# A retention kernel with two MLPs behind it: query multiplications and decay tables issued a block ahead, a converted piece's parts a block behind

## The chip, the cores and the metric

The kernel runs on one core of a Trainium2 chip. The metric is the device time of one execution in microseconds (us), the median of several. PE is the matrix engine, DVE the vector engine, ACT the scalar engine, POOL the GpSimd engine; SP only issues transfers.

## What is computed

The reference, cut to its core:

```
def _attn_ref(q, k, v):                      # 2 x 8 heads x 768 x 64, fp32
    gamma = 1.0 - 2.0 ** (-5.0 - np.arange(H))
    for t in range(S):
        state = gamma * state + einsum('bhd,bhe->bhde', k[:, :, t], v[:, :, t])
        y[:, :, t] = scale * einsum('bhd,bhde->bhe', q[:, :, t], state)

x = y.transpose(0, 2, 1, 3).reshape(1536, 512)
x = ((x @ w_a) * (x @ w_b)) @ w_out          # d_ff 1536
h = x @ w_in                                 # d_ff 2048
out = (h * sigmoid(1.702 * h)) @ w_out2
```

The weights come as float64 and the kernel converts them to two float32 parts (hi and lo); activations are split in two parts as well, and each product is the sum of three.

## The kernel before

**Retention.** The two sequences of 768 rows are cut into 12 blocks of 128 rows, `SEQ` = 6 to a sequence. For block n the kernel does this:

- `att_load(n)`: two transfers of 512 KB on SP's queue, `qv` (queries, values) and `kk` (keys in two layouts). Four buffers (`RAWBUFS`) each; iteration n issues the load of block n+4, and in some iterations also a 512 KB weight piece (`w_dma`).
- `att_q(n)`: POOL multiplies the queries with a decay table `qdec[c]`, c = n % 6. Table 1 is loaded; the others are made from it by `att_qdec(c)`, four ACT instructions with the factors `gdec[c]`, which POOL writes at the start with 64x1 memsets.
- `att_v(n)`: POOL multiplies the values with `vdec[c]`.
- `att_scores(n)`: PE, `ps_sc` from `kk` and q; then DVE masks them into `a`.
- `att_kv(n)`: PE adds block n's keys times values to `ps_kv`; then ACT copies that to `state`. The last block of a sequence has none.
- `att_av(n)`: PE, `a` times v (L204) and, except in a sequence's first block, `state` times q (L216); then ACT rounds the result to `xh`, and DVE takes the rest to `xl`.

Each engine runs its instructions in the order in which the program issues them (the schedule is manual). In iteration n that order is: scores(n+1), v(n+1), kv(n), the decay table of block n+2, one conversion step, av(n), q(n+2), the load of block n+4.

**Conversion during the retention.** Three weight pieces (`EARLY`) are converted in blocks 2 to 10, one step to a block: `w_bits`, `w_sign`, `w_add` on DVE, and with the third step `w_parts`: ACT rounds `wt` to `wh`, POOL takes the rest to `wl`.

**Start.** 11 small products on zeros (`warm`) keep PE occupied until the first data, then scores(0), then 8 more. Block 0's load is cut into four transfers of 256 KB, which go, with the decay tables and the mask, to SP's and ACT's queues.

**MLPs.** `layer(1)` and `layer(2)` follow; their first product (L342) is issued right behind the last av. Nothing in them is touched.

The buffers' waits come from the framework. Transfers take turns on eight completion semaphores, so that one is issued only when the eighth before it has landed.

Of the kernel before, what the change touches and what calls it, by code (L numbers as in the profile page):

```python
# [7 lines left out]
F32 = mybir.dt.float32  # L8
# [5 lines left out]
ALU = mybir.AluOpType  # L14

P = 128
B, H, S, D = 2, 8, 768, 64
NP = H // 2
# [6 lines left out]
SEQ = S // P  # L25
# [15 lines left out]
def retention_moe_kernel(  # L41
# [9 lines left out]
    nc = tc.nc  # L51
# [9 lines left out]
    attp = retention.enter_context(tc.tile_pool(name="attp", bufs=2))  # L61
    ps_att = retention.enter_context(tc.tile_pool(name="ps_att", bufs=1, space=PSUM))

    def lo_part(engine, lo, src, hi):
        engine.tensor_tensor(out=lo, in0=src, in1=hi.bitcast(F32), op=ALU.subtract)  # L65
# [5 lines left out]
    causal = attp.tile([P, 1, P], F32, tag="causal", name="causal", bufs=1)  # L71
# [9 lines left out]
    def att_load(n):  # L81
        if n >= NBLK:
            return
        qv, kk = (attp.tile([P, 2, DM], F32, tag=t, name=t, bufs=RAWBUFS) for t in ("qv", "kk"))
        if n == 0:
            nc.sync.dma_start(out=qv[:, 0, :], in_=att[n][:, 0, :])
            nc.scalar.dma_start(out=kk[:, 0, :], in_=att[n][:, 1, :])
            nc.scalar.dma_start(out=causal[:, 0, :], in_=cmask[:, 0:P])
            nc.scalar.dma_start(
                out=vdec[:, 0].rearrange("p h o -> p (h o)"), in_=cdec[:, NP * P:NP * P + H]  # L90
            )
            nc.sync.dma_start(out=qv[:, 1, :], in_=att[n][:, 3, :])
            nc.scalar.dma_start(out=kk[:, 1, :], in_=att[n][:, 2, :])
            nc.scalar.dma_start(out=qdec[:, 1].rearrange("p a t -> p (a t)"), in_=cdec[:, 0:NP * P])
        else:
            nc.sync.dma_start(out=qv, in_=att[n][:, 0:4:3, :])
            nc.sync.dma_start(out=kk, in_=att[n][:, 1:3, :])
        qv_t[n], kk_t[n] = qv, kk

    def att_constants():  # L100

        gamma = [1.0 - 2.0 ** (-5.0 - h) for h in range(H)]
        for c in range(1, SEQ):
            for h in range(H):
                nc.gpsimd.memset(vinv[:, c, h, :], gamma[h] ** (-float(P) * c))  # L105
        for c in range(SEQ):
            for h in range(H):
                rows = slice(64 * (h % 2), 64 * (h % 2) + 64)
                nc.gpsimd.memset(gdec[rows, c, h // 2:h // 2 + 1], gamma[h] ** (float(P) * (c - 1)))  # L109

    def att_vdec():

        nc.vector.tensor_scalar(
            out=causal, in0=causal, scalar1=0.0, scalar2=1.0, op0=ALU.is_gt, op1=ALU.mult
        )
        for c in range(1, SEQ):
            nc.gpsimd.tensor_tensor(out=vdec[:, c], in0=vdec[:, 0], in1=vinv[:, c], op=ALU.mult)  # L117

    def att_qdec(c):

        if c < SEQ and c != 1:
            for p in range(NP):
                nc.scalar.activation(
                    out=qdec[:, c, p], in_=qdec[:, 1, p], func=ACTF.Copy, scale=gdec[:, c, p:p + 1]
                )

    def att_q(n):
        if n < NBLK:
            t = attp.tile([P, NP, P], F32, tag="q", name="q", bufs=3)
            (nc.vector if n == 1 else nc.gpsimd).tensor_tensor(  # L130
                out=t, in0=qv_t[n][:, 0, :].rearrange("p (a t) -> p a t", t=P), in1=qdec[:, n % SEQ], op=ALU.mult
            )
            q_t[n] = t

    def att_v(n):
        if n < NBLK:
            t = attp.tile([P, H, D], F32, tag="v", name="v")
            nc.gpsimd.tensor_tensor(  # L138
                out=t,
                in0=qv_t[n][:, 1, :].rearrange("p (h d) -> p h d", d=D),  # L140
                in1=vdec[:, n % SEQ].to_broadcast([P, H, D]),
                op=ALU.mult,
            )
            v_t[n] = t
# [53 lines left out]
    def att_av(n):  # L198
        c = n % SEQ
        ps = ps_att.tile([P, NP, P], F32, tag="av", name="ps_av", bufs=2)  # L200
        for p in range(NP):
            for h2 in range(2):
                h = 2 * p + h2
                nc.tensor.matmul(  # L204
                    ps[64 * h2:64 * h2 + 64, p, :],
                    v_t[n][:, h, :],
                    a_t[n][:, NP * h2 + p, :],
                    start=(p == 0),
                    stop=(c == 0),
                    skip_group_check=True,  # L210
                )
        if c > 0:
            for p in range(NP):
                for h2 in range(2):
                    rows = slice(64 * h2, 64 * h2 + 64)
                    nc.tensor.matmul(  # L216
                        ps[rows, p, :],
                        state_t[n][rows, p, :],
                        q_t[n][rows, p, :],
                        start=False,  # L220
                        stop=True,
                        skip_group_check=True,
                    )
        hi, lo = (t[:, :, n * P:(n + 1) * P] for t in x)
        if n == 0:
            t = attp.tile([P, NP, P], F32, tag="q", name="x0", bufs=3)
            nc.vector.tensor_tensor(out=t, in0=ps, in1=qdec[:, 0], op=ALU.mult)
            ps = t
        nc.scalar.copy(hi, ps)
        lo_part(nc.vector, lo, ps, hi)  # L230
# [10 lines left out]
    is_down = [j == 3 - ph for ph, f, j in pieces]  # L241
    wraw, wt, whl = {}, {}, {}
    nxt = {"dma": 0, "split": 0}
    room = {False: WUP, True: WDOWN}
    stage = [None, None, None]

    def w_dma():
        i = nxt["dma"]
        if i >= len(pieces):
            return  # L250
        nxt["dma"] += 1
        ph, f, j = pieces[i]
        t = rawp.tile([P, DM, 2], I32, tag="wraw", name="wraw", bufs=4)
        src = (w1 if ph == 1 else w2)[f][:, j, :]
        nc.sync.dma_start(out=t.rearrange("p a b -> p (a b)"), in_=src.bitcast(I32))
        wraw[i] = t
# [3 lines left out]
    def w_carry(i):  # L260
        low, high = wraw[i][:, :, 0], wraw[i][:, :, 1]
        wt[i] = rawp.tile([P, DM], F32, tag="wt", name="wt", bufs=3)
        nc.scalar.activation(out=wt[i], in_=high.bitcast(F32), func=ACTF.Abs)  # L263
        nc.scalar.activation(out=low, in_=low.bitcast(U32), func=ACTF.Copy, scale=2.0 ** -29)  # L264
# [19 lines left out]
    def w_parts(i):  # L284
        t = wt.pop(i)
        pool = wdown if is_down[i] else wup
        whl[pieces[i]] = hi, lo = [pool.tile([P, DM], F32R, tag=x, name=x) for x in ("wh", "wl")]
        nc.scalar.copy(hi, t)  # L288
        lo_part(nc.gpsimd, lo, t, hi)
# [18 lines left out]
    def w_early(n):  # L308

        i, k = divmod(n - 2, 3)  # L310
        if i < 0 or i >= EARLY:
            return
        (w_bits, w_sign, w_add)[k](i)
        if k == 2:
            w_dma()
            w_parts(i)
            room[is_down[i]] -= 1
            nxt["split"] += 1

    def w_points(n):  # L320
        for _ in range(n):
# [137 lines left out]
    def warm(ps, n):  # L459

        for _ in range(n):
            nc.tensor.matmul(ps[:, 0, :], zero, zero, start=True, stop=True)

    with tc.manual_schedule():
        nc.vector.memset(zero, 0.0)
        att_constants()
        for n in range(RAWBUFS):
            att_load(n)
        ps = ps_att.tile([P, NP, P], F32, tag="av", name="ps_warm", bufs=2)
        warm(ps, WARM)  # L470
        att_v(0)
        att_vdec()
        att_scores(0)
        att_q(1)
        warm(ps, 8)
        for n in range(NBLK):
            if n > 0:
                att_scores(n + 1)
            att_v(n + 1)
            att_kv(n)  # L480
            if n < SEQ:
                att_qdec(n + 2 if n else 0)
                if n == 0:
                    att_qdec(2)
            w_early(n)
            att_av(n)
            if n == 0:
                att_scores(1)
            att_q(n + 2)
            if n + RAWBUFS < NBLK:  # L490
                att_load(n + RAWBUFS)
            if n in (0, 1, 2, 9):
                w_dma()
            if n % 3 == 1 and n // 3 < EARLY:
                w_carry(n // 3)
        layer(1)
        layer(2)
# [66 lines left out]
```

## Time and profile before

| | us |
|---|---|
| Median of 3 runs | 626.16 (625.23 to 626.41) |
| The profiled execution's own time | 626.12 |
| Its span | 624.3 |
| PE busy in the span | 607.0 (97%) |
| DVE, ACT, POOL busy | 371.7, 237.1, 150.0 |
| First product of the MLPs starts at | 64.09 |

The span is what the profiler saw between the first and the last instruction; 1.8 us of the execution's own time lie around it. In the chain of work that ended last, PE has 93% and POOL 3%. The busy share is a mean over stages: the stage that the change touches is the retention, the first 64 us.

### The profile page before, as it was taken

The numbers are of one execution on the slowest core, as the hardware profiler recorded it, in microseconds if no ns is written. First come the engines' busy times: TensorE is split into PE (matmuls) and PEld (weight loads), VectorE is DVE, ScalarE is ACT, GpSimd is POOL, SyncE is SP. The second block draws the span as 40 slices with busy tenths as digits, with TensorE's granted clock in tenths as the row PEclk, the third lists the DMA queues.
The fourth block names the chain that finished last, engine by engine and source line by source line (L and its number), as shares of the span: only waits on it lengthen the run. The fifth ranks groups of instructions, "written<-read, shape, count | busy, mean of one in ns | idle before, by whom it ended". The sixth has DMA issues, their size and how long they took to land.

```text
span 624.3 us, 7868 instructions
## 1 busy us (share of the span) xinstructions
PE 607.0 (97%) x3190; PEld 504.9 (81%) x3190; DVE 371.7 (60%) x414; ACT 237.1 (38%) x340; POOL 150.0 (24%) x187
## 2 busy tenths in 40 slices
PE   7888999999999999999999999999999999999996
PEld 6777888888888888888888888888888888888885
DVE  3554268776056777235887667842888377836422
ACT  2433244444134552034444265534554055314300
POOL 7455033323012323002332212220223022202000
PEclk9888999999999999999999999999999999999999
DMA  8973123225012333012331212131114102200022
GB/s 311 369 244 111 35 77 97 97 71 166 0 35 68 101 102 101 1 34 68 101 102 34 69 34 68 62 107 35 63 39 135 35 34 68 67 1 1 0 101 102
DMA packets 17043, 52.21 MB, mean 84 GB/s; under 512 B 1776, under 2 KB 1904, under 8 KB 17008
## 3 DMA queue, kind: packets, MB, share of 16 engines
q1 hardware_dynamic: 16288, 50.86, 24.9%
q10 hardware_dynamic: 720, 0.86, 0.4%
q8 instruction: 25, 0.41, 0.3%
q14 instruction: 10, 0.08, 0.0%
HBM read 48.57 MB, written 3.15 MB: 83 GB/s over the span
## 4 chain that ended last, share of the span: by engine, by line
PE 93%; POOL 3%; issue 3%; DVE 0%; DVEq 0%; POOLq 0%
PE ps L342 52%; PE ps L379 37%; PE ps_sc L159 1%; PE ps_av L204 1%; PE ps_av L216 1%; POOL v L138 1%; POOL q L130 1%; POOL gdec L109 1%; PE ps_kv L186 1%; POOL vinv L105 0%; DVE part L396 0%; POOL vdec L117 0%; DVEq L560 0%; POOL wl L65 0%; POOLq L138 0%
## 5 line engine op out<-in xcount | busy, mean ns | idle before, releaser
L65 POOL TENSOR_TENSOR wl<-wt,wh 128x512 fp32r<-128x512 f32 x68 | 117.0, 1725 | 410.1 <-ACT wh L288 385.1
L342 PE MATMUL ps<-xh,wh 128*128 128x512 f32 x480 | 128.9, 389 | 0.0
L342 PE MATMUL ps<-xl,wh 128*128 128x512 f32 x480 | 128.8, 389 | 0.0
L342 PE MATMUL ps<-xh,wl 128*128 128x512 f32 x480 | 128.8, 389 | 0.0
L342 PEld LDWEIGHTS ps<-xl,wh 128*128 128x128 f32 x480 | 90.1, 188 | 18.7
L342 PEld LDWEIGHTS ps<-xh,wh 128*128 128x128 f32 x480 | 90.0, 188 | 18.8 <-issue 0.2
L342 PEld LDWEIGHTS ps<-xh,wl 128*128 128x128 f32 x480 | 90.1, 188 | 18.7
L269 DVE TENSOR_SCALAR wt<-wt 128x512 f32<-128x512 f32 x68 | 63.8, 938 | 53.5 <-ACT wt L263 53.5
L359 ACT CAST gh<-sb 128x1536 fp32r<-128x1536 f32 (+1 forms) x42 | 44.1, 1051 | 112.6 <-DVE sb L358 106.2
L358 DVE TENSOR_TENSOR sb<-ps,sb 128x1536 f32<-128x1536 f32 (+1 forms) x42 | 51.3, 1220 | 48.8 <-ACT sb L442 24.4
L65 DVE TENSOR_TENSOR gl<-sb,gh 128x1536 fp32r<-128x1536 f32 (+1 forms) x42 | 51.5, 1226 | 47.1 <-ACT gh L359 47.1
L396 DVE TENSOR_TENSOR part<-ps,part 128x1536 f32<-128x1536 f32 (+1 forms) x24 | 35.5, 1487 | 48.4 <-PE ps L379 48.4
L288 ACT CAST wh<-wt 128x512 fp32r<-128x512 f32 x68 | 42.0, 617 | 42.1 <-DVE wt L282 42.1
L276 DVE SCALAR_TENSOR_TENSOR wt<-wraw,wt 128x512 int32<-128x512 int32 x68 | 55.7, 819 | 2.2
L379 PE MATMUL ps<-wl,gh 128*128 128x512 f32 x192 | 55.2, 389 | 0.0
L379 PE MATMUL ps<-wh,gh 128*128 128x512 f32 x192 | 55.2, 389 | 0.0
L379 PE MATMUL ps<-wh,gl 128*128 128x512 f32 x192 | 55.2, 389 | 0.0
L282 DVE CUSTOM_DVE_ANT_0 wt<-wraw,wt 128x1024 uint16<-128x1024 uint16 x68 | 50.6, 744 | 6.4
L263 ACT ACTIVATE wt<-wraw 128x512 f32<-128x512 f32 x68 | 45.7, 672 | 1.5 <-POOL wl L65 1.5
L264 ACT ACTIVATE wraw<-wraw 128x512 int32<-128x512 uint32 x68 | 45.2, 664 | 0.0
L442 ACT ACTIVATE sb<-ps 128x1536 f32<-128x1536 f32 (+1 forms) x24 | 23.8, 1029 | 54.1 <-PE ps L342 54.1
L436 ACT COPY sb<-ps 128x1536 f32<-128x1536 f32 x12 | 17.4, 1446 | 66.6 <-PE ps L342 66.6
(47 smaller groups left out, 559.9 us busy)
## 6 DMA issues: line engine op xcount, KB each, us to landing
wraw<-in_w_dram SPq DMA_DIRECT2D x68, 512.0 KB, 3.7
qv<-in_att_dram SPq DMA_DIRECT2D x11, 512.0 KB, 7.1
kk<-in_att_dram SPq DMA_DIRECT2D x11, 512.0 KB, 6.0
out_dram<-part SPq DMA_DIRECT2D x3, 768.0 KB, 3.6
out_dram<-part SPq DMA_DIRECT2D x3, 256.0 KB, 2.1
kk<-in_att_dram ACTq DMA_DIRECT2D x2, 256.0 KB, 5.2
qv<-in_att_dram SPq DMA_DIRECT2D x2, 256.0 KB, 4.4
qdec<-in_cdec_dram ACTq DMA_DIRECT2D x1, 256.0 KB, 6.3
```

The lines of the kernel that those rows point to most:

```text
L65: engine.tensor_tensor(out=lo, in0=src, in1=hi.bitcast(F32), op=ALU.subtract)
L263: nc.scalar.activation(out=wt[i], in_=high.bitcast(F32), func=ACTF.Abs)
L264: nc.scalar.activation(out=low, in_=low.bitcast(U32), func=ACTF.Copy, scale=2.0 ** -29)
L269: nc.vector.tensor_scalar(out=t, in0=t, scalar1=F64_LOW, scalar2=F64_HIGH, op0=ALU.max, op1=ALU.min)
L276: nc.vector.scalar_tensor_tensor(out=ti, in0=wraw[i][:, :, 1], scalar=-0x40000000, in1=ti, op0=ALU.bitwise_and, op1=ALU.bitwise_or)
L282: nc.vector.tensor_tensor(out=ti, in0=ti, in1=wraw.pop(i)[:, :, 0], op=ALU.add)
L288: nc.scalar.copy(hi, t)
L342: nc.tensor.matmul(ps[:, g, :], l, r, start=(i == 0 and k == 0), stop=(i == 2 and k == max(late or now)), skip_group_check=True,)
L358: nc.vector.tensor_tensor(out=sb[:, c], in0=ps[:, c], in1=sb[:, c], op=ALU.mult)
L359: nc.scalar.copy(gh[:, c], sb[:, c])
L379: nc.tensor.matmul(ps[:, n, :], l, r, start=(f == min(g_t) and i == 0), stop=(f == max(g_t) and i == 2), skip_group_check=True,)
L396: nc.vector.tensor_tensor(out=t[:, c], in0=ps[:, c], in1=t[:, c], op=ALU.add)
```

## The change

Nearly the same instructions are issued in another order.

- q(n+2) is issued ahead of v(n+1) and kv(n), not behind av(n), and the decay table of block n+3, not n+2, is made in iteration n. Table 2 is made before the loop, ahead of the first `state` copy on ACT.
- The tag `q` gets 4 buffers for 3, `v` 3 for 2.
- `gdec` is written in the order 2, 0, 3, 4, 5; table 1's 8 memsets are left out, since it is loaded. Only vdec 1 is made ahead of v(1), the other four behind q(2).
- `w_parts(i)` is issued one block behind `w_add(i)`, ahead of that block's av.
- The second half of block 0's `kk` goes to SP's queue, not ACT's.
- The second warm-up has 12 products, not 8.

```
             nc.sync.dma_start(out=qv[:, 1, :], in_=att[n][:, 3, :])
-            nc.scalar.dma_start(out=kk[:, 1, :], in_=att[n][:, 2, :])
+            nc.sync.dma_start(out=kk[:, 1, :], in_=att[n][:, 2, :])
...
-        for c in range(SEQ):
+        for c in (2, 0, 3, 4, 5):
...
-            t = attp.tile([P, NP, P], F32, tag="q", name="q", bufs=3)
+            t = attp.tile([P, NP, P], F32, tag="q", name="q", bufs=4)
...
-            t = attp.tile([P, H, D], F32, tag="v", name="v")
+            t = attp.tile([P, H, D], F32, tag="v", name="v", bufs=3)
...
         i, k = divmod(n - 2, 3)
+        if i > 0 and k == 0:
+            w_parts(i - 1)
+            room[is_down[i - 1]] -= 1
+            nxt["split"] += 1
         if i < 0 or i >= EARLY:
             return
         (w_bits, w_sign, w_add)[k](i)
         if k == 2:
             w_dma()
-            w_parts(i)
-            room[is_down[i]] -= 1
-            nxt["split"] += 1
...
-        att_vdec()
+        att_vdec([1])
...
         att_q(1)
-        warm(ps, 8)
+        att_qdec(2)
+        warm(ps, 12)
         for n in range(NBLK):
             if n > 0:
                 att_scores(n + 1)
-            att_v(n + 1)
+            if n == 0:
+                att_v(1)
+                att_q(2)
+                att_vdec(range(2, SEQ))
+            else:
+                att_q(n + 2)
+                att_v(n + 1)
             att_kv(n)
-            if n < SEQ:
-                att_qdec(n + 2 if n else 0)
-                if n == 0:
-                    att_qdec(2)
+            if n == 0:
+                att_qdec(0)
+            if n + 3 < SEQ:
+                att_qdec(n + 3)
             w_early(n)
             att_av(n)
             if n == 0:
                 att_scores(1)
-            att_q(n + 2)
```

ACT from its first computing instruction to block 1, before (`state` is the copy behind kv, L123 the decay tables, four instructions to a table, `xh` the rounding behind av):

```order
L195 ACT_TABLE_LOAD
L195 COPY state_251<-ps_kv_242 128x256
L123 ACTIVATE qdec_83<-qdec_83,gdec_82 128x128 x8
L229 CAST xh_85<-x0_270 128x4x128
L195 COPY state_314<-ps_kv_242 128x256
L123 ACTIVATE qdec_83<-qdec_83,gdec_82 128x128 x4
L229 CAST xh_85<-ps_av_320 128x4x128
```

The same place after the change (L120 are the decay tables, L192 the copy, L226 the rounding):

```order
L120 ACT_TABLE_LOAD
L120 ACTIVATE qdec_83<-qdec_83,gdec_82 128x128 x4
L192 COPY state_253<-ps_kv_244 128x256
L120 ACTIVATE qdec_83<-qdec_83,gdec_82 128x128 x8
L226 CAST xh_85<-x0_272 128x4x128
L192 COPY state_316<-ps_kv_244 128x256
L120 ACTIVATE qdec_83<-qdec_83,gdec_82 128x128 x4
L226 CAST xh_85<-ps_av_322 128x4x128
```

Four instructions (table 2) and the table load now stand ahead of the first copy of the state; the eight behind it are tables 0 and 3, where they were 0 and 2.

POOL from block 4 to the first converted piece, before (`qv_287`, `qv_341`, `qv_400` and `qv_455` are blocks 4, 5, 6 and 7; `wl_486` is the first piece's second part):

```order
L130 TENSOR_TENSOR q_398<-qv_287,qdec_83 128x512
L138 TENSOR_TENSOR v_417<-qv_287,vdec_80 128x512
L130 TENSOR_TENSOR q_453<-qv_341,qdec_83 128x512
L138 TENSOR_TENSOR v_470<-qv_341,vdec_80 128x512
L65 TENSOR_TENSOR wl_486<-wt_347,wh_485 128x512
L130 TENSOR_TENSOR q_508<-qv_400,qdec_83 128x512
L138 TENSOR_TENSOR v_528<-qv_400,vdec_80 128x512
L130 TENSOR_TENSOR q_551<-qv_455,qdec_83 128x512
```

After (`qv_287`, `qv_341`, `qv_400`, `qv_451` and `qv_502` are blocks 4 to 8):

```order
L127 TENSOR_TENSOR q_417<-qv_341,qdec_83 128x512
L135 TENSOR_TENSOR v_419<-qv_287,vdec_80 128x512
L127 TENSOR_TENSOR q_466<-qv_400,qdec_83 128x512
L135 TENSOR_TENSOR v_468<-qv_341,vdec_80 128x512
L127 TENSOR_TENSOR q_520<-qv_451,qdec_83 128x512
L135 TENSOR_TENSOR v_522<-qv_400,vdec_80 128x512
L65 TENSOR_TENSOR wl_525<-wt_347,wh_524 128x512
L127 TENSOR_TENSOR q_564<-qv_502,qdec_83 128x512
```

Each q stands one block further ahead of the v beside it, and the piece's part stands behind the q of block 7, where it stood ahead of the q of block 6.

## Rows read from the trace of the kernel before

**Rows 1.** Waits in 0 to 66 us: us in total, times, longest.

```profile
PE ps_sc L159 <- POOL q L130: 10.2, 6, 2.8
```

**Rows 2.** Timeline, late retention: start us, us, engine, line, operation [idle before <-releaser].

```profile
40.76 1.16 PE L159 MATMUL ps_sc<-q,kk 64*128 64x128 f32 x16
43.34 1.16 PE L159 MATMUL ps_sc<-q,kk 64*128 64x128 f32 x16
...
54.84 1.16 PE L159 MATMUL ps_sc<-q,kk 64*128 64x128 f32 x16
...
56.45 1.05 PE L204 MATMUL ps_av<-a,v 128*64 128x128 f32 x16
...
58.44 1.16 PE L159 MATMUL ps_sc<-q,kk 64*128 64x128 f32 x16
...
64.09 1.20 PE L342 MATMUL ps<-xh,wh 128*128 128x512 f32 x4
```

**Rows 3.** Timeline, block 2 of the retention.

```profile
20.19 1.16 PE L159 MATMUL ps_sc<-q,kk 64*128 64x128 f32 x16 [0.26 <-POOL q L130]
...
22.34 1.28 ACT L123 ACTIVATE qdec<-qdec,gdec 128x128 f32<-128x128 f32 x4
...
23.70 1.27 POOL L130 TENSOR_TENSOR q<-qv,qdec 128x512 f32<-128x512 f32 x1 [2.55 <-ACT qdec L123]
...
24.53 0.69 DVE L65 TENSOR_TENSOR xl<-ps_av,xh 128x512 fp32r<-128x512 f32 x1 [1.11 <-ACT xh L229]
...
25.02 1.16 PE L159 MATMUL ps_sc<-q,kk 64*128 64x128 f32 x16 [1.15 <-POOL q L130]
```

**Rows 4.** Timeline, POOL at the first converted piece.

```profile
33.60 1.27 POOL L65 TENSOR_TENSOR wl<-wt,wh 128x512 fp32r<-128x512 f32 x1 [2.81 <-ACT wh L288]
```

**Rows 5.** Windows: busy us by engine (instructions), granted clock, DMA share, GB/s.

```profile
16.00:17.00 1.00, 1.00 (x20) 0.92 (x19) 1.00 (x2) 0.00 (x0) 0.11 (x1) 0.50 1.03 414
20.00:30.00 10.00, 7.51 (x130) 6.44 (x132) 5.84 (x8) 6.05 (x15) 4.89 (x6) 1.00 1.00 357
```

**Rows 6.** Timeline, the first two blocks.

```profile
3.29 1.28 ACT L195 ACT_TABLE_LOAD   x1 [3.29 <-issue]
...
6.77 2.05 PE L462 MATMUL ps_warm<-zero 128*128 128x128 f32 x16
...
9.07 1.29 DVE L130 TENSOR_TENSOR q<-qv,qdec 128x512 f32<-128x512 f32 x1 [0.96 <-DMA qdec<-in_cdec_dram]
...
9.87 0.69 PE L186 MATMUL ps_kv<-v,kk 128*64 128x64 f32 x16 [1.05 <-POOL v L138]
...
13.86 1.35 DVE L65 TENSOR_TENSOR xl<-x,xh 128x512 fp32r<-128x512 f32 x1 [0.98 <-ACT xh L229]
...
14.71 1.44 PE L159 MATMUL ps_sc<-q,kk 64*128 64x128 f32 x16 [2.19 <-POOL q L130]
15.13 2.34 DVE L167 TENSOR_TENSOR a<-ps_sc,causal 128x1024 f32<-128x1024 f32 x2
...
16.99 1.92 PE L204 MATMUL ps_av<-a,v 128*64 128x128 f32 x16
```

**Rows 7.** Timeline of SP's queue: three loads.

```profile
5.39 0.43 SPq L96 DMA_DIRECT2D qv<-in_att_dram  x1
...
7.18 0.53 SPq L97 DMA_DIRECT2D kk<-in_att_dram  x1
...
22.39 0.42 SPq L255 DMA_DIRECT2D wraw<-in_w_dram  x1
```

**Rows 8.** The same three in DMA views of their own: KB, us to landing.

```profile
qv<-in_att_dram SPq DMA_DIRECT2D x1, 512.0 KB, 6.2
...
kk<-in_att_dram SPq DMA_DIRECT2D x1, 512.0 KB, 9.4
...
wraw<-in_w_dram SPq DMA_DIRECT2D x1, 512.0 KB, 6.4
```

**Rows 9.** The page: a conversion step on DVE (busy, mean ns).

```profile
L276 DVE SCALAR_TENSOR_TENSOR wt<-wraw,wt 128x512 int32<-128x512 int32 x68 | 55.7, 819 | 2.2
```

More of the change, by code (lines that the diff above doesn't have):

```diff
@@ L109, in att_constants, with att_vdec @@
                 nc.gpsimd.memset(gdec[rows, c, h // 2:h // 2 + 1], gamma[h] ** (float(P) * (c - 1)))
[L111 to L116, printed above, removed]
+    def att_vdec(cs):
+        for c in cs:
             nc.gpsimd.tensor_tensor(out=vdec[:, c], in0=vdec[:, 0], in1=vinv[:, c], op=ALU.mult)
@@ L225, in att_av @@
         if n == 0:
-            t = attp.tile([P, NP, P], F32, tag="q", name="x0", bufs=3)
+            t = attp.tile([P, NP, P], F32, tag="q", name="x0", bufs=4)
             nc.vector.tensor_tensor(out=t, in0=ps, in1=qdec[:, 0], op=ALU.mult)
@@ L471, in retention_moe_kernel @@
         att_v(0)
-        att_vdec()
+        att_vdec([1])
+        nc.vector.tensor_scalar(
+            out=causal, in0=causal, scalar1=0.0, scalar2=1.0, op0=ALU.is_gt, op1=ALU.mult
+        )
         att_scores(0)
         att_q(1)
-        warm(ps, 8)
+        att_qdec(2)
+        warm(ps, 12)
         for n in range(NBLK):
```

## The prediction

> **What bounds the kernel now.** I read the chain of work that ended last first: nearly all of it is PE (the table above). So time can only come from stretches in which PE waits, or runs at the lower level of its clock. The waits of the first 66 us come next: six times PE waits for POOL's q ahead of the scores, 10.2 us in total [rows 1]. The timeline of the retention then shows three kinds of blocks; q(n), sc(n), kv(n), av(n) and so on are block n's.
>
> Late blocks run at PE's own pace: from sc(10) at 54.84 to sc(11) at 58.44 is 3.60 us; a block without the product with the state takes 43.34 - 40.76 = 2.58; from sc(11) to the first MLP product at 64.09 it is 5.65 [rows 2]. A block without kv I put at 3.0: 3.60 less 0.6, the kv row of 0.69 without its drain [rows 6].
>
> Blocks 3 to 5 are slower: from 20.19 to 25.02 is 4.83 us [rows 3]. The reader is to see a closed loop there: sc starts, kv follows, ACT copies the state and only then makes the next table (22.34, 1.28 us), POOL's q starts when that is done after idling 2.55, and PE's next sc starts when q is done after idling 1.15. PE's 3.6 us of work are part of a loop of 4.8.
>
> The third kind follows a converted piece: POOL idles 2.81 us for `wh`, with the next q queued behind that wait [rows 4]; PE's longest wait for a q is 2.8 [rows 1].
>
> The clock comes on top. Between 16 and 17 us the granted clock is 0.50, the 1.2 GHz level, after PE idled 2.19 us ahead of sc(2) [rows 5, 6]; from 20 to 30 us, with idle times of 1.15, it is 1.00, the 2.4 GHz level. The part L204 of av takes 1.92 us at the lower level [rows 6] and 1.05 at the upper [rows 2].
>
> The transfers are the next thing in line: from 20 to 30 us the DMA engines' share is 1.00 [rows 5]. kk(3) is issued at 7.18 and lands 9.4 later, at 16.58; the third weight piece is issued at 22.39 and lands 6.4 later, at 28.79 [rows 7, 8]. In SP's order that is the ninth transfer of 512 KB behind kk(3), so one takes (28.79 - 16.58) / 9 = 1.36 us.
>
> **The start.** ACT now loads its function table and makes decay table 2 ahead of the first state copy, and this waits for the loaded table 1. Before, DVE waited for that table until 9.07 [rows 6]. Were it still so, the copy could start at 9.07 + 1.28 (function table) + 1.28 (four activations) = 11.63; before, it started when kv(0), which started at 9.87, was through, about 10.6. That would be 1.0 us late. But `kk`'s half, 256 KB, no longer stands ahead of table 1 in ACT's queue, which at the rate above is worth 0.68 us: I take 11.63 - 0.68 = 10.95, 0.3 late, with bounds of 0 and 1.0. The Trainium skill has a rule against this (DMA: Bandwidth & Descriptors, section "Issuing engines are not separate DMA queues"): all issuers' transfers interleave on the same 16 engines, and another issuer saves only the issuing time. By that rule the gain here is one issue, some 0.4 us, and the copy 0.6 late; no run yet tells which. The final sum by it would be at most 0.3 us longer.
>
> SP's queue gets the half: qv(1) comes one issue and 0.68 us of transfer later. q(1), on DVE, waited for table 1 anyway, and sc(1) stands behind av(0), which ends near 9.87 + 0.5 + 1.05 = 11.4; q(1) would be ready near 10.4, a cover of 1 us. The four added warm-up products cost 4 x 2.05 / 8 = 1.0 us, which fits PE's wait ahead of kv(0), 1.05 us [rows 6]; the omitted memsets let POOL's v(0) come earlier, so the cover holds and kv(0) stays at 9.87.
>
> q(2) now stands ahead of the remaining vdec work and waits for qv(2), which lands at 5.39 + 6.2 = 11.59 [rows 7, 8] and for table 2 at 10.95: it ends at 11.65 + 1.27 = 12.92. kk(2), one transfer behind qv(2), lands at 12.95, and sc(2) starts then instead of at 14.71. PE does kv(1) and is through at 12.95 + 1.16 + 0.6 = 14.7. Next it needs a(1). Before, DVE started a(1) at 15.13 (two of them in 2.34 us) [rows 6], at the end of the sequence state copy, table 0, x0, xh(0), xl(0), which is not shortened: a(1) is ready at 15.13 + 1.17 + 0.3 = 16.6. That is the stall that takes over: PE idles 1.9 us and av(1) starts at 16.65, not 16.99.
>
> Does the clock fall here? 1.15 us of idling left it up, 2.19 let it fall; 1.9 is nearer to the second. I take the lower level for av(1): before, it took from 16.99 until PE went idle at 20.19 - 0.26, 2.94 [rows 3, 6]. So sc(3) is at 19.6, against 20.19 before; with the clock up av takes 3.60 - 1.16 - 0.6, some 1.9, and sc(3) is at 18.6.
>
> **Blocks 3 to 11.** Table c is made two iterations ahead of its sc and q one, so the loop of 4.8 is open; POOL's own work per block is 1.27 for q and, with v taken at the same, 2.5 in all, under 3.6. PE's pace then gives: sc(4) 23.2, sc(5) 26.8, sc(6) 30.4; block 5 has no kv, sc(7) 33.4; block 6 has no product with the state, sc(8) 36.0.
>
> The floor under it is the landing of kk. kk(4) to kk(8) are the 2nd, 5th, 8th, 11th and 14th transfer behind kk(3) (two weight pieces and more lie between): 19.3, 23.4, 27.5, 31.5, 35.6. Each is just ahead of PE. With the clock up from sc(3) PE would be at sc(8) at 35.0 and wait for 35.7. So both branches meet: sc(8) near 36.0. From there 3 x 3.60 + 5.65 = 16.45 to the first MLP product: 52.4, against 64.09.
>
> **The converted pieces.** `wh` is issued when its `wt` has been ready for a block, so POOL's wait of 2.81 is gone; `wl`'s own 1.27 us stay, hidden in POOL's slack of 3.6 - 2.5 and the block that q now lies ahead. Without that cover a block with a piece would cost 1.3 more. The third piece's rounding now precedes xh(11) on ACT, some 0.6 us later; the last columns of x are read last by the first MLP product, which hides it. The extra buffers cost nothing.
>
> **The sum.** The MLPs do what they did, shifted by 64.09 - 52.4 = 11.7 us. The profiled execution's 626.12 less 11.7 is 614.4 (its span 624.3 becomes 612.6); it lies at the median of the runs, so that stands for the median too.
>
> **Rivals.**
> Transfers slower: from 20 to 30 us the engines moved 357 GB/s [rows 5], which makes 1.47 us for 524,288 bytes. Then kk(8) lands at 16.58 + 14 x 1.47 = 37.2, the MLPs start at 53.7, and the time is 615.7; if freed PE time makes the loads bunch, up to 617.
>
> DVE and POOL in each other's way: xl(0), whose inputs lie in SBUF, took 1.35 us beside a q of POOL's [rows 6], xl(2), from PSUM, 0.69 [rows 3]. POOL now works while DVE does the conversion steps. DVE has 1.17 + 0.69 + 0.82 [rows 9] = 2.68 us to do in a block; if each step waits a whole q it is 3.95, 0.35 over PE's pace, in nine blocks 3.2: 617.6. That needs the step to fall at the worst place each time. The Trainium skill (SBUF — State Buffer, section "SBUF: two separate sides") makes this an exclusive lock that the later of the two waits out; the 1.35 agrees.
>
> More low clock: a new stall of over 2 us elsewhere costs up to 1.9 (sc(2) to sc(3) took 5.48 instead of 3.60 before): 616.3, two of them 618.2.
>
> Slower than before: the short waits for kk in every block could hold the clock down throughout. A block then takes 3.60 x 1.92 / 1.05 = 6.6 us, 3.0 more; with four such blocks the gain is gone, with all of 3 to 11 the time is 641. Against it: 20 to 30 us had a wait in each block and stayed at 1.00.
>
> No change: POOL's q could wait for qv with v behind it and rebuild a loop of 4.8. But sc(n+2) needs that q ahead of kv(n+1), which needs the v; and the v behind that q, at most its 1.27, runs beside sc's 1.16.
>
> **How the numbers follow.** 60% for 614.4 (its own range 613.0 to 615.3: the PE branch without the DMA floor, and the copy 1.0 late); 14% for slower transfers, 10% for DVE and POOL, 8% for more low clock; 4% slower than before, 4% no change. Within 0.2% (1.25 us, about what a measurement of this kernel can tell) are only the last; so 0.92 faster, 0.04 the same, 0.04 slower. The range of 612.8 to 618.2 takes in the first four.
>
> **What would show it.** Right: sc(2) near 13 and av(1) near 16.6, blocks 3, 4 at 3.6 to 4.1 us, no wait of POOL's for a table from block 3 on, kk landing within 2 us of its sc up to block 8, the first MLP product near 52.4, the MLPs' length unchanged. Wrong: POOL or DVE ending PE's waits in the middle blocks, the clock at 0.50 past block 2, or kk(8) landing past 37.5.

## The result and the profile after

| | before | after |
|---|---|---|
| Median of 4 runs, us | 626.18 (625.23 to 626.41) | 615.62 (614.26 to 616.34) |
| The profiled execution's own time | 626.12 | 614.94 |
| Its span | 624.3 | 613.2 |
| First product of the MLPs starts at | 64.09 | 52.91 |

The ratio is 0.9832, with a 95% interval of 0.9809 to 0.9854: 1.7% faster. The forecast was 614.4 in a range of 612.8 to 618.2.

The profiled execution's MLPs start 64.09 - 52.91 = 11.18 us earlier, and 626.12 - 11.18 = 614.94 is its own time: the whole gain lies ahead of the first MLP product. In the page of after the chain that ended last is now PE's to 97% (it was 93%, with 3% for POOL):

```profile
span 613.2 us, 7880 instructions
...
PE 604.5 (99%) x3198; PEld 502.8 (82%) x3198; DVE 374.6 (61%) x414; ACT 236.9 (39%) x340; POOL 149.9 (24%) x179
...
PE 97%; DMA 2%; DVE 0%; POOL 0%; DVEq 0%; SPq 0%; issue 0%; POOLq 0%
```

The waits of after from 0 to 56 us (us in total, times, longest), those that answer to [rows 1] and [rows 4]:

```profile
POOL wl L65 <- ACT wh L285: 4.9, 2, 4.3
POOL q L127 <- DMA qv<-in_att_dram: 4.3, 7, 1.5
POOL q L127 <- ACT qdec L120: 3.0, 2, 2.3
...
PE ps_sc L156 <- POOL q L127: 1.5, 1, 1.5
...
PE ps_sc L156 <- DMA kk<-in_att_dram: 1.1, 1, 1.1
```

PE's six waits for q, 10.2 us, have become one of 1.5. That one is ahead of sc(2). POOL itself still waits for tables, transfers and `wh`, but behind sc(2) PE waits for POOL nowhere.

PE's timeline after, from sc(3) on (start, us, engine, line, operation):

```profile
19.91 1.16 PE L156 MATMUL ps_sc<-q,kk 64*128 64x128 f32 x16
...
23.51 1.16 PE L156 MATMUL ps_sc<-q,kk 64*128 64x128 f32 x16
...
27.11 1.16 PE L156 MATMUL ps_sc<-q,kk 64*128 64x128 f32 x16
...
30.72 1.16 PE L156 MATMUL ps_sc<-q,kk 64*128 64x128 f32 x16
...
33.85 1.16 PE L156 MATMUL ps_sc<-q,kk 64*128 64x128 f32 x16
...
36.44 1.16 PE L156 MATMUL ps_sc<-q,kk 64*128 64x128 f32 x16
...
52.91 1.20 PE L340 MATMUL ps<-xh,wh 128*128 128x512 f32 x4
```

These answer to [rows 2, 3]: from sc(3) to sc(6) a block takes 3.60 us, where the loop of 4.8 was, and no row has an idle time in front of it. From sc(6) to sc(7) (block 5 has no kv) it is 3.13, from sc(7) to sc(8) (block 6 has no product with the state) 2.59, and from sc(8) to the MLPs 16.47.

The first two blocks after, which answer to [rows 6]; the number in brackets is the engine's idle time before the row and what ended it:

```profile
9.99 1.28 ACT L120 ACT_TABLE_LOAD   x1 [9.99 <-DMA qdec<-in_cdec_dram]
...
10.60 0.69 DVE L127 TENSOR_TENSOR q<-qv,qdec 128x512 f32<-128x512 f32 x1 [2.40 <-DMA qv<-in_att_dram]
...
12.47 0.35 ACT L192 COPY state<-ps_kv 128x256 f32<-128x256 f32 x1
...
13.28 1.26 POOL L127 TENSOR_TENSOR q<-qv,qdec 128x512 f32<-128x512 f32 x1 [1.09 <-DMA qv<-in_att_dram]
...
14.60 1.95 PE L156 MATMUL ps_sc<-q,kk 64*128 64x128 f32 x16 [1.50 <-POOL q L127]
...
15.70 0.69 DVE L65 TENSOR_TENSOR xl<-x,xh 128x512 fp32r<-128x512 f32 x1 [0.98 <-ACT xh L226]
15.91 1.62 POOL L127 TENSOR_TENSOR q<-qv,qdec 128x512 f32<-128x512 f32 x1 [0.72 <-DMA qv<-in_att_dram]
16.31 2.35 DVE L164 TENSOR_TENSOR a<-ps_sc,causal 128x1024 f32<-128x1024 f32 x2
...
17.59 1.37 PE L201 MATMUL ps_av<-a,v 128*64 128x128 f32 x16
```

Here the forecast is off: ACT's table load, which waits for decay table 1, starts at 9.99 and not at 9.07 - 0.68 = 8.39, and sc(2) at 14.60, not 12.95. The q that sc(2) waits for has itself waited for qv(2), not for table 2. The windows (busy us of PE, PEld, DVE, ACT, POOL with their instructions, granted clock, DMA share, GB/s) show the clock at its lower level behind PE's two waits, and at the upper level for good by 20 us:

```profile
15.00:16.00 1.00, 1.00 (x14) 1.00 (x12) 0.30 (x1) 0.67 (x2) 0.28 (x3) 0.50 1.03 391
...
17.00:18.00 1.00, 1.00 (x16) 0.82 (x14) 1.00 (x2) 0.35 (x2) 1.00 (x2) 0.50 1.03 408
18.00:19.00 1.00, 1.00 (x18) 0.83 (x16) 0.66 (x1) 1.00 (x5) 0.53 (x1) 0.90 1.02 395
...
20.00:30.00 10.00, 10.00 (x182) 8.78 (x184) 7.15 (x10) 5.13 (x12) 6.36 (x6) 1.00 1.02 394
```

The last row answers to [rows 5]: PE is busy for all 10 us, where it was 7.51, and the transfers move 394 GB/s, where it was 357.

### The profile page after: what moved, and what is told of

It is laid out like the page before. It is cut to its first block, busy times and chain, and to the rows that moved or that the text cites. A ratio compares the mean times of both kernels' runs of the same rounds, so it can differ in the third digit from the quotient of the medians.

```text
span 613.2 us, 7880 instructions
## 1 busy us (share of the span) xinstructions
PE 604.5 (99%) x3198; PEld 502.8 (82%) x3198; DVE 374.6 (61%) x414; ACT 236.9 (39%) x340; POOL 149.9 (24%) x179
## 4 chain that ended last, share of the span: by engine, by line
PE 97%; DMA 2%; DVE 0%; POOL 0%; DVEq 0%; SPq 0%; issue 0%; POOLq 0%
PE ps L340 53%; PE ps L377 37%; PE ps_sc L156 2%; PE ps_av L201 2%; PE ps_av L213 2%; DMA qv<-in_att_dram 1%; PE ps_kv L183 1%; DMA kk<-in_att_dram 1%; DVE part L394 0%; POOL q L127 0%; DVEq L567 0%; SPq L97 0%; POOLq L127 0%
## 5 line engine op out<-in xcount | busy, mean ns | idle before, releaser
L266 DVE TENSOR_SCALAR wt<-wt 128x512 f32<-128x512 f32 x68 | 65.3, 960 | 53.5 <-ACT wt L260 53.5
L273 DVE SCALAR_TENSOR_TENSOR wt<-wraw,wt 128x512 int32<-128x512 int32 x68 | 57.5, 846 | 2.2
```

Of the source, the lines that this page charges most:

```text
L266: nc.vector.tensor_scalar(out=t, in0=t, scalar1=F64_LOW, scalar2=F64_HIGH, op0=ALU.max, op1=ALU.min)
L273: nc.vector.scalar_tensor_tensor(out=ti, in0=wraw[i][:, :, 1], scalar=-0x40000000, in1=ti, op0=ALU.bitwise_and, op1=ALU.bitwise_or)
```

## The experiments

In the names below sc(n), q(n), a(n) and av(n) are block n's, as in the prediction. Times are medians with the lowest and highest run; ratios are to the kernel before, run beside them.

### Which part of the change brings the gain

**e5_tables_and_q_only.** The kernel before with the decay tables and q a block ahead, and their buffers; the start's transfers, `gdec`, vdec, the warm-up and the pieces' parts as before. (The order of q alone can't be tried: the table has to be issued ahead of the q that reads it.)

```
+        att_qdec(2)
...
-            att_v(n + 1)
+            if n == 0:
+                att_v(1)
+                att_q(2)
+            else:
+                att_q(n + 2)
+                att_v(n + 1)
             att_kv(n)
-            if n < SEQ:
-                att_qdec(n + 2 if n else 0)
...
+            if n == 0:
+                att_qdec(0)
+            if n + 3 < SEQ:
+                att_qdec(n + 3)
...
-            att_q(n + 2)
```

> The kernel before with two parts of the change: tables and q a block ahead (with the buffers that q and v need for it). No part moved behind its step, no edit of the start's loads, memsets, vdec work or warm-up. Theory (these two parts are the change; the rest is worth nothing here): blocks 3 to 11 at 3.6 us, POOL's wait for wh off PE's path, 614.5 to 616.0. Rival (the start or the parts carry a share): 618 to 620.

614.67 us (613.86 to 616.31), ratio 0.9820 (0.9802 to 0.9837): as fast as the whole change. These two reorderings are what the change brings; the rest together adds nothing that can be measured with runs that lie some 2 us apart.

**e2_tables_ahead_only.** The kernel before with the tables ahead, q left behind av.

```
         att_q(1)
+        att_qdec(2)
...
-            if n < SEQ:
-                att_qdec(n + 2 if n else 0)
-                if n == 0:
-                    att_qdec(2)
+            if n == 0:
+                att_qdec(0)
+            if n + 3 < SEQ:
+                att_qdec(n + 3)
```

> The kernel before with one part of the change: table 2 ahead of the loop, table n+3 in iteration n. Theory (blocks 3 to 5 are a loop through the table, and only that): those blocks fall from 4.8 to about 3.6 us, POOL never waits for a table from block 4 on, the waits for wh stay (2.6 and 2.8 us of PE's, and the low clock behind each): 3 us gained, 623. Rival (q has to stand ahead of v as well before the loop opens): blocks 3 to 5 stay at 4.8 us, 626.

622.44 (620.78 to 622.91), ratio 0.9938 (0.9917 to 0.9958). sc(3), sc(4) and sc(5) start at 18.73, 22.33 and 25.93: the loop of 4.8 is open at 3.60, and the edit alone is worth 626.14 - 622.44 = 3.7 us. Of these 20.19 - 18.73 = 1.46 lie ahead of sc(3): table 2, made before the loop, brings sc(2) from 14.71 to 13.22. Then comes the first converted piece, POOL's and PE's timeline:

```profile
29.82 1.28 POOL L65 TENSOR_TENSOR wl<-wt,wh 128x512 fp32r<-128x512 f32 x1 [3.64 <-ACT wh L288]
31.05 1.27 POOL L130 TENSOR_TENSOR q<-qv,qdec 128x512 f32<-128x512 f32 x1
...
32.38 1.90 PE L159 MATMUL ps_sc<-q,kk 64*128 64x128 f32 x16 [2.77 <-POOL q L130]
```

q stands behind `wl` in POOL's queue, `wl` behind `wh`, so PE idles 2.77 us and its scores then take 1.90, not 1.16: the clock has fallen (0.50 from 33 to 36 us). The second piece does the same at 46.13. The other two thirds of the gain come from here.

**e3_parts_behind_only.** The kernel before with `w_parts` one block behind `w_add`, nothing else.

```
+        if i > 0 and k == 0:
+            w_parts(i - 1)
...
         if k == 2:
             w_dma()
-            w_parts(i)
```

> The kernel before with one part of the change: a piece's two parts one block behind its third conversion step. Theory (PE's two long waits and the low clock after them come from POOL waiting for wh with q queued behind): both waits and both low stretches go, 2.7 + 1.6 and 2.8 + 1.5 us, 8 us in all, 618; blocks 3 to 5 stay at 4.8. Rival (the wait only moves to the next block, since POOL then does wl ahead of q for 1.3 us): 1 to 3 us gained, 623 to 625.

623.49 (622.50 to 624.99, 12 runs), ratio 0.9965 (0.9951 to 0.9979). From sc(3) to sc(5) a block keeps its 4.82 us. POOL's timeline, with PE's row behind it:

```profile
36.53 1.26 POOL L65 TENSOR_TENSOR wl<-wt,wh 128x512 fp32r<-128x512 f32 x1 [2.11 <-ACT wh L288]
37.75 1.45 POOL L130 TENSOR_TENSOR q<-qv,qdec 128x512 f32<-128x512 f32 x1
...
39.24 1.16 PE L159 MATMUL ps_sc<-q,kk 64*128 64x128 f32 x16 [1.95 <-POOL q L130]
```

The wait is not gone, it has moved a block on and shrunk: `wh` is still issued in the block of its `wl`, behind that block's work on ACT. The rival is right; what the theory forecast of this edit by itself is not reached.

**e4_parts_behind_undone.** The changed kernel with `w_parts` back where it was.

```
-        if i > 0 and k == 0:
-            w_parts(i - 1)
...
         if k == 2:
             w_dma()
+            w_parts(i)
```

> The changed kernel with one edit undone: a piece's parts are issued right behind its third conversion step again. Theory (a q that lies a block ahead hides POOL's wait for wh by itself, so that this edit is only a second cover): POOL waits up to 2 us for wh, but PE's blocks stay at 3.6: 615.6 to 616.1. Rival (each edit carries its own share): PE waits for q again at two blocks, 619 to 621.

614.86 (614.41 to 616.64), ratio 0.9829 (0.9804 to 0.9853): nothing lost. Its waits:

```profile
POOL wl L65 <- ACT wh L285: 5.1, 3, 2.6
...
PE ps_sc L156 <- POOL q L127: 0.9, 4, 0.3
```

POOL waits for `wh` as ever, 5.1 us; PE feels at most 0.3 of it, since the next q already stands ahead. So q a block ahead is what hides the pieces, not the deferral.

**e9_buffers_undone.** The changed kernel with 3 buffers for `q` and 2 for `v`, as before.

```
-            t = attp.tile([P, NP, P], F32, tag="q", name="q", bufs=4)
+            t = attp.tile([P, NP, P], F32, tag="q", name="q", bufs=3)
...
-            t = attp.tile([P, H, D], F32, tag="v", name="v", bufs=3)
+            t = attp.tile([P, H, D], F32, tag="v", name="v", bufs=2)
```

> The changed kernel with the fourth buffer of q and the third of v taken back. Theory (the buffers are free when POOL wants them, since av of two blocks earlier is done): 615 to 616.3, as with the change. Rival (a v a block ahead has to wait for av of the block before, with the next q behind it on POOL): PE waits for q in several blocks, 617 or more.

614.79 (614.07 to 615.36), ratio 0.9832 (0.9817 to 0.9847): the added buffers are worth nothing that can be measured here.

### The start

**e1_kk_half_on_act.** The changed kernel with the half of `kk` back on ACT's queue.

```
-            nc.sync.dma_start(out=kk[:, 1, :], in_=att[n][:, 2, :])
+            nc.scalar.dma_start(out=kk[:, 1, :], in_=att[n][:, 2, :])
```

> The changed kernel with one edit undone: the second half of block 0's kk goes to ACT's queue again, ahead of table 1. Theory (that move is what made the first transfers land 1 to 2.6 us later: table 1 at 9.94 for 8.95, qv(1) at 10.5 for 7.86, qv(2) at 13.15 for 11.59): they land as in the kernel before, sc(2) starts at 13.0 to 13.4 instead of 14.60, av(1) near 17.2, and the MLPs near 52.3, 0.6 earlier than with the change: about 615.0. Rival (the later landings come from elsewhere, or vary from run to run): landings and time as with the change, 615.6.

615.79 (615.71 to 615.99), ratio 0.9839 (0.9816 to 0.9861): no faster than the changed kernel. The theory's landings came: the table load started at 8.81, the state copy at 11.29, sc(2) at 12.82. Its time did not, which went into another wait; the timeline:

```profile
14.14 1.27 POOL L127 TENSOR_TENSOR q<-qv,qdec 128x512 f32<-128x512 f32 x1 [0.74 <-DMA qv<-in_att_dram]
14.53 1.44 DVE L65 TENSOR_TENSOR xl<-x,xh 128x512 fp32r<-128x512 f32 x1 [0.98 <-ACT xh L226]
15.89 2.34 DVE L164 TENSOR_TENSOR a<-ps_sc,causal 128x1024 f32<-128x1024 f32 x2
...
17.16 1.09 PE L201 MATMUL ps_av<-a,v 128*64 128x128 f32 x16 [2.56 <-DVE a L164]
...
19.98 1.99 PE L156 MATMUL ps_sc<-q,kk 64*128 64x128 f32 x16
```

The windows of e1 behind that wait (columns as above):

```profile
19.00:20.00 1.00, 1.00 (x12) 0.67 (x9) 0.00 (x0) 0.00 (x0) 0.11 (x1) 0.50 1.06 397
...
21.00:22.00 1.00, 1.00 (x12) 0.86 (x12) 0.40 (x1) 0.84 (x2) 0.00 (x0) 0.63 1.02 406
```

Two things are to be seen. q(3) now starts ahead of xl(0), and xl(0), whose inputs lie in SBUF, takes 1.44 us where it took 0.69 after: it ends 0.56 behind q(3). And PE, done earlier, idles 2.56 for a(1); behind it the clock is at the lower level until 21 to 22 us.

**e11_after_again.** The changed kernel, unchanged, for a second profile: three kernels that share its start had shown earlier landings than its first profile.

> The changed kernel once more, for a second profile of its start. Theory (the late start was that execution's own): in the first profile ACT's function table load, which waits for decay table 1, began at 9.99; in three kernels that keep the half of kk on SP's queue it began at 8.68, 9.02 and 9.20, in the kernels with the half on ACT's queue at 8.80 to 9.59. Then it begins at 8.7 to 9.3 here, q(1) before 9.6, sc(2) at 12.9 to 13.5. Rival (the half on SP's queue makes the table late in this kernel): the load begins at 9.8 or later again, sc(2) past 14. The time: 614.2 to 616.4 by both.

614.06 (613.94 to 616.40), ratio 0.9818 (0.9795 to 0.9841). The table load starts at 9.46, between what the theory and the rival said; sc(2), at 14.07, comes as late as the rival had it. The timeline:

```profile
9.46 1.28 ACT L120 ACT_TABLE_LOAD   x1 [9.46 <-DMA qdec<-in_cdec_dram]
...
15.17 0.69 DVE L65 TENSOR_TENSOR xl<-x,xh 128x512 fp32r<-128x512 f32 x1 [0.98 <-ACT xh L226]
15.38 1.61 POOL L127 TENSOR_TENSOR q<-qv,qdec 128x512 f32<-128x512 f32 x1 [0.72 <-DMA qv<-in_att_dram]
...
17.05 1.09 PE L201 MATMUL ps_av<-a,v 128*64 128x128 f32 x16 [1.21 <-DVE a L164]
...
19.10 1.16 PE L156 MATMUL ps_sc<-q,kk 64*128 64x128 f32 x16
...
52.09 1.21 PE L340 MATMUL ps<-xh,wh 128*128 128x512 f32 x4
```

Table 1 by kernel, as the start of ACT's load: with the half on SP's queue 8.68 (e4), 9.02 (e9), 9.20 (e10), 9.46 (e11) and 9.99 (after); on ACT's, with the load in the same place, 8.80 (e8), 8.81 (e1, e7), 9.01 (e6), 9.09 (e2) and 9.59 (e5). The two lists overlap, their medians are 9.20 and 8.91. The table did not come 0.68 earlier with the move; whether it comes some 0.3 later can't be told from these. qv(1), which now stands behind the half, is what q(1) waits for last in all five kernels of the first list (9.03 to 10.60), and in none of the second. The same holds for q(2) and qv(2).

### The lower clock and the transfers

**e6_warm_fill.** e1 with nine small products on zeros ahead of av(1), in PE's longest wait.

```
             w_early(n)
+            if n == 1:
+                warm(ps, 9)
             att_av(n)
```

> The kernel of e1 with 9 more products on zeros behind kv(1), where PE idles 2.56 us for a(1). Theory (the clock falls because of that idling, and costs about 0.9 us in av(1) and 0.8 in sc(3)): granted clock 1.00 through 17 to 22 us, av(1) at the same place, sc(3) 0.9 and sc(4) 1.6 us earlier, 1.6 us off the time unless the landing of kk(8) takes some back: 614.2 to 615.2, for e1's 615.8. Rival (the low clock has another cause): the clock falls all the same, 615.8.

614.39 (614.12 to 614.69), ratio 0.9813 (0.9799 to 0.9826). The clock is at 1.00 from 14 us on, sc(4) starts at 23.02 (e1: 24.41), the MLPs at 52.40 (53.79). av(1) itself starts at 17.37, later than in e1: the 1.4 us are the clock's alone.

**e7_sc1_first.** e1 with sc(1) ahead of av(0).

```
             w_early(n)
+            if n == 0:
+                att_scores(1)
             att_av(n)
-            if n == 0:
-                att_scores(1)
```

> The kernel of e1 with scores(1) issued ahead of av(0), so that DVE makes a(1) ahead of x0 and xl(0). Theory (a(1) behind xl(0) on DVE is what PE waits for in block 1): PE's 2.56 us of idling goes, the clock stays at 1.00, sc(3) at 16.5 for 19.98; then the landing of kk is the next limit, kk(8) at 35 to 36, so that 1.5 to 2 of the 5 us reach the end: 613.7 to 614.5. Rival (the landing of kk sets nothing up to block 8): all of it reaches the end, 610.8 to 611.5.

614.01 (613.87 to 614.10), ratio 0.9806 (0.9792 to 0.9819). a(1) is done ahead of the state copy's chain, so the stall is gone: av(1) starts at 14.44, sc(3) at 16.70, 3.3 us ahead of e1. At the MLPs it is 53.79 - 51.97 = 1.8 ahead, of which e6 puts 1.4 down to the clock. PE's and POOL's timeline show where the rest of the 3.3 went:

```profile
16.70 1.16 PE L156 MATMUL ps_sc<-q,kk 64*128 64x128 f32 x16 [0.20 <-DMA kk<-in_att_dram]
...
22.13 0.69 PE L183 MATMUL ps_kv<-v,kk 128*64 128x64 f32 x16 [0.66 <-ACT state L192]
...
33.83 1.27 POOL L127 TENSOR_TENSOR q<-qv,qdec 128x512 f32<-128x512 f32 x1
...
35.15 1.16 PE L156 MATMUL ps_sc<-q,kk 64*128 64x128 f32 x16 [1.11 <-POOL q L127]
```

qv(8) is issued at 25.53 and lands 8.2 later, at 33.73; q(8) starts at 33.83 and PE waits 1.11 for it. kk(8) lands at 26.00 + 9.0 = 35.0. The transfers are the floor now. They are also behind the wait of 0.66 at kv(3): the state copy stands on ACT behind the first conversion step, which had waited 3.36 us for its weight piece.

**e8_sc1_first_late_pieces.** e7 with the weight pieces of iterations 1 and 2 issued in 3 and 8.

```
-            if n in (0, 1, 2, 9):
+            if n in (0, 3, 8, 9):
```

> The kernel of e7 with the loads of the second to fifth weight piece issued later (in iterations 3, 4, 7 and 8 instead of 1, 2, 4 and 7), so that one piece instead of three or four lies ahead of kk(5) to kk(7), and three instead of four ahead of kk(8). Theory (the transfers are the floor under blocks 5 to 8): 1 to 2.5 us less than e7, 611.5 to 613. Rival (PE's own order is the floor): the same as e7.

613.19 (612.97 to 613.40), ratio 0.9793 (0.9780 to 0.9806), the fastest of all, 0.8 under e7, where the theory had 1 to 2.5. kk(8) lands at 26.14 + 7.5 = 33.64, 1.36 earlier; sc(8) starts at 34.23 without a wait of note, the MLPs at 51.05, 0.9 earlier. So PE had stood on the transfers there. The wait for the state copy at kv(3), 0.67 here, is left.

**e10_late_pieces.** The changed kernel with the same move of the pieces (the edit shown under e8), without e7's edit.

> The changed kernel with the loads of the second to fifth weight piece issued later, as in e8, and nothing else. Theory (in the changed kernel, after its low clock in blocks 1 and 2, PE reaches sc(8) at 36.4, when kk(8) has just landed, so that the transfers take nothing): 615 to 616, as with the change. Rival (they are its floor already): 1 us or more off, 614.5 or less in the median.

616.92 (613.80 to 620.00, 6 runs), ratio 0.9866 (0.9839 to 0.9894). The median is above both forecasts and 2.1 above e9's, run beside it: no gain is shown, and the runs lie further apart than any other kernel's. In its profile xl(0) took 1.50 beside q(3), PE idled 2.55 for a(1) and the clock was at 0.50 from 18 to 20 us; sc(3) came at 21.00. Why its runs spread by 6 us stays open.

## Why the prediction was right

**The loop of 4.8 and the pace of 3.60: right.** e2 shows the tables' part of it, e5 the whole; in the changed kernel no wait of PE's is left from sc(3) on.

**The converted pieces: right that the wait of 2.81 no longer costs anything, wrong in the reason.** The prediction said that `wh` is issued when its `wt` has been ready for a block, "so POOL's wait of 2.81 is gone". It is not: POOL waits 4.9 us for `wh` after the change. e3 shows that the deferral alone only moves the wait, e4 that without it nothing is lost. What hides it is the cover that the prediction named second, the q that lies a block ahead.

**The start: the term "worth 0.68 us" for the half of `kk` was wrong.** Table 1 was there at 8.68 to 9.99 us in the five profiles with that edit, in none of them 0.68 ahead of the 9.07 of before. The rule that the prediction weighed against it, the Trainium skill's (DMA: Bandwidth & Descriptors, "Issuing engines are not separate DMA queues"), gave one issue, some 0.4 us. The table's issue is indeed 0.5 earlier (2.14 after, 2.63 in e1); its landing is not, so the sum by that rule was the nearer one, and even its gain is not to be seen. The bytes went ahead of qv(1) instead, and q(1) waits for that. They also stand ahead of qv(2), which the prediction left at 11.59: it landed at 11.60 to 13.16 in these five, and q(2), and with it sc(2), waited for it in each. sc(1) was held up too, by kk(1): 1.06 us in the first profile, 0.55 in e11. The state copy started at 11.16 (e4) to 12.47 (after), not at 10.95, and sc(2) at 13.03 to 14.60, not at 12.95.

**Why that cost so little: the stall for a(1).** It was forecast at 1.9 us, with av(1) at 16.65. It measured 1.47 to 1.51 in e4 and e9, 1.21 in e11, and none in the first profile, whose sc(2) came so late that PE was not idle there any more; e10, with the same start, had 2.55. In the four others av(1) started at 16.28, 16.62, 17.05 and 17.59: it hangs on the chain behind the state copy, and a late sc(2) only takes time out of that wait. The chain from the copy's start to a(1)'s start takes 3.84 to 3.86 us in these four, not the 15.13 - 10.60 = 4.53 of before [rows 6], because POOL's q (q(2) before, now q(3)) starts behind xl(0) and not ahead of it; in e1, e5, e6 and e10, where q(3) starts first, xl(0) takes 1.40 to 1.50 and the chain 4.56 to 4.66. So e1's state copy came 1.18 us earlier than the first profile's, and its a(1) only 0.42.

**DVE and POOL in each other's way: it happens, and off the path.** Besides xl(0) it shows behind the first piece; DVE's timeline after, beside `wl` of POOL's at 33.16 and q at 34.67:

```profile
33.19 1.52 DVE L266 TENSOR_SCALAR wt<-wt 128x512 f32<-128x512 f32 x1
34.74 1.49 DVE L267 TENSOR_SCALAR wt<-wt 128x512 int32<-128x512 int32 x1
```

The same two took 0.41 and 0.43 at 22.38 and 22.83, with POOL idle. Each waits out one POOL instruction and no more, as the Trainium skill has it (SBUF — State Buffer, "SBUF: two separate sides": an exclusive lock for a whole instruction). PE waited for none of them; the rival's 617.6 needed one such wait in every block.

**The clock: right as a branch, not as a certainty.** The prediction took the lower level for av(1) and put sc(3) at 19.6, or 18.6 with the clock up. Both came: 19.91 after, with the clock down; 18.66 in e9, 18.33 in e4 and 19.10 in e11, with the clock at 1.00 throughout. e10 was beyond both, with the longer stall, the clock down behind it and sc(3) at 21.00. In the first profile the clock did not fall where the prediction had it, at the wait for a(1), but ahead of it, behind the waits for kk(1) and q(2), and it rose again while block 1's av ran (0.90 from 18 to 19 us). So av(1) came 17.59 - 16.65 = 0.94 late and took 2.32 us to sc(3) instead of 2.94: that sc(3) was still within 0.3 of the forecast is two errors that cancel, and luck.

**The floor and the sum: right in size.** kk(8) was forecast to land at 35.6; it landed at 28.32 + 7.5 = 35.8 after, and at 35.3 to 35.6 in e4, e9 and e11. sc(8) was forecast near 36.0 by either branch: 36.44 after, 35.57, 35.73 and 35.63 in the others. The clock-up branch was to wait there for kk(8); in e11 PE came at that time by its own pace, without a wait. That the floor is real for a PE that comes earlier, e7 and e8 show; in the changed kernel e10 got nothing from moving the pieces. From sc(8) to the MLPs 16.45 was forecast, 16.47 measured. The shift of the MLPs, 11.7 in the forecast, was 11.18 in the first profile and 64.09 - 52.09 = 12.00 in the second. The median of the first four runs is 1.2 us above the forecast, that of all eight, 614.60, 0.2: the range held them all.

## What to carry to other kernels

Where an engine's wait closes a loop over three engines, issue the producer a block ahead of every slower step in its own queue: that opens the loop, and it also hides what later lands in that queue, so that a second edit made for that purpose is worth nothing. Before crediting an edit with an earlier transfer, ask what the same bytes now stand ahead of. And when a stall is removed, look up the next two in line: here the chain behind the state copy and, behind that, the transfers; e7 took the one, e8 both: 614.01 and 613.19 us. Of the changed kernel's eight runs, with 614.60 as their median, the faster ones (613.94 to 614.26) are as fast as e7's; only e8's (up to 613.40) lie below all eight.

## What the runs showed of the hardware

**The same idle time may or may not bring the clock down.** PE idled 2.56 us in e1, and the clock was at 0.67 and 0.50 from 18 to 21 us; 2.54 in e5, and it stayed at 1.00; two waits of 1.06 and 1.50 in the first profile of after brought it down, 0.55, 1.51 and 1.21 in e11 did not. e5's windows behind the wait:

```profile
17.00:18.00 1.00, 0.10 (x2) 0.10 (x4) 1.00 (x2) 0.00 (x0) 1.00 (x2) 1.00 1.05 416
18.00:19.00 1.00, 1.00 (x18) 0.83 (x20) 0.97 (x1) 0.00 (x0) 1.00 (x2) 1.00 1.00 387
```

The times of one kernel's runs go with the clock, if not exactly. The changed kernel's eight are 613.94, 613.96, 614.15, 614.26 and 614.94, and 616.29, 616.34 and 616.40, the last three with a mean granted clock of 0.995 or 0.996, the first four with 0.998 or 1.0; 614.94 lies between with 0.996. The kernels without the long idle time, e6, e7 and e8, have all their runs within 0.6 us; so has e1, at the lower mean clock in all four (0.995 or 0.996). What decides it was not found.

**The first transfers vary from execution to execution.** Decay table 1, issued at the same 2.14 to 2.15 us in five executions of kernels with the same start, was there for ACT between 8.68 and 9.99 us.
